# Moving the ranked stages of a sorted attention pair against its ranking chain in a routed-attention and feed-forward kernel

## The chip, the cores and the metric

The kernel runs on one core of a Trainium2 chip. The number that counts is the device time of one execution in microseconds (us); the median of three executions before the change is 958.43 us, the lowest 957.55 and the highest 960.12. The engines of the core are called by their short names in the profile: PE multiplies matrices (and transposes, by a product with an identity), PEld loads the stationary operand for it, DVE is the vector engine, ACT the scalar engine, POOL the GpSimd engine, and SP issues most transfers. Each works through its own list of instructions; they wait for one another through semaphores.

## The reference

A routed attention is followed by a feed-forward block. A query and a key see one another only when they fall into the same one of 16 clusters; the cluster of a row is the argmax of its products with the normalised centroids.

```
q_assign = argmax(einsum('bhsd,hcd->bhsc', q_n, c_n), -1)      # B, H, S, D = 4, 8, 768, 64; 16 clusters
k_assign = argmax(einsum('bhsd,hcd->bhsc', k_n, c_n), -1)
scores = where(q_assign == k_assign, q @ k^T / 8, -1e9)
attn = softmax(scores);  x = attn @ v                           # then (B, H, S, D) -> (B*S, H*D) = 3072 x 512
h = x @ w_in;  g = h * clip(h + 3, 0, 6) / 6;  out = g @ w_out  # w_in 512 x 2048, w_out 2048 x 512
```

## The kernel before

The 32 heads are worked as 16 pairs of heads, `g` = 0 to 15. Pairs 0 to 7 are attended in full, with a mask; this and the decoding of the weights is the first part of the kernel and takes about 255 us. Pairs 8 to 15 are sorted by cluster first, so that only a band of blocks next to the diagonal has to be computed. The change touches only this second part.

**The feed-forward work** is cut into blocks of 256 tokens, three to a batch. A block has eight `up` items and seven `down` items, and each item has two halves, so a block is 30 halves. The first half of an `up` item (`begin`, the `uX` products) ends with two additions on DVE; the second (`uY`) with three additions into `g_sb`, after which `finish` clips the item before it (L502) and, for every second one, forms four sums of the clipped tiles (`gated_sums`, L635), which in this part of the kernel run on DVE. A `tx` transfer (L548) brings the weight sums for the item two further on. A half of a `down` item is eight products of 256 columns. All halves stand in one list, `fill`, in order, and this list never runs empty while the sorted pairs are worked.

**The plan.** The order of the work is written out by hand. `late_plan` lays out a row of points. At each point, `point` in the loop at L1325, the steps planned for it are issued first and then one half from `fill`, except at the two points of a pair that are called busy (L1328). A point with an `up` or `down` half is thus the unit in which the plan counts. Pair `g` has its own zero at point 38 + 28 (g - 8), so one pair follows another at a distance of 28 points (`SLOT`), and `steps_of` (L1172 to L1196) gives each step its offset to this zero. Steps of two neighbouring pairs interleave: offset -30 of one pair is offset -2 of the pair before. At one point, the steps of the earlier pair come first.

**The steps of a pair**, in the order of the work:

- `load_natural`, `turn_natural`: queries and keys are loaded in their natural order (the tile `piece`) and transposed on PE (L899), ACT copies the result (L900).
- The ranking chain: `cluster_scores` (L337, product and copy), `own_clusters` (three transposes `pr` on PE, then `mx` and `oh` on DVE), `run_up` (six small DVE additions), `step_up` (four DVE additions, the last into `upto`), `order` (ten small products into `rk` on PE, the first of which read `upto`; then `edges` and `prod` on DVE) and `positions` (`posf`, `pos` on DVE: the place of each row in its sorted head).
- `load_queries`, `load_keys`: natural rows again, for `scatter`. `scatter` (L1014) is 24 indirect transfers on POOL, each followed by three small memsets (`pause`), which write the rows of queries, keys and values to their places in memory (`qd`, `kvd`).
- `load_ranked` (L870 for queries and keys into `piece`, L893 for values into `vs`) reads the sorted rows back by SP's queue. `turn_ranked` transposes them (again L899 and L900, into `xsort`). `band_masks` makes the mask of the band on DVE (three instructions).
- `band_scores`, `band_values`, `key_adds`, `band_sums`, `band_divide`: the band attention, up to `xr` on DVE (L1144).
- `keep_ranked` stores `xr` to `xsd` by SP's queue; `gather` (L1030), 12 indirect transfers on POOL, fetches the rows back in their natural order into `xn`; `turn_back` transposes them and stores them to `xd`. After the last pair of a batch `turn_back` also puts the batch's feed-forward blocks on `fill` and, when the buffer is free, starts the load `xb` of the next block. `token_sums` (L575) forms sums of `xb` on DVE before the block's first `up`.

All `turn` steps, the band scores and `band_divide` use the one buffer `ps` of PSUM. After the plan comes a check of ranges on DVE (`whether_good`), and then what is left of `fill`.

Of the kernel before, what the change touches and what calls it, by code (L numbers as in the profile page):

```python
# [119 lines left out]
def fast_path(ctx, tc, ok, q, k, v, centroids, moe_w_in, moe_w_out, out):  # L120
# [68 lines left out]
    def load(g, *names):  # L189
        if g > FIRST or (g == FIRST and "v" in names):  # L190
            return
        b, h = divmod(2 * g, H)
        for name in names:
            if name == "v":
                dst = st["v", g] = vp.tile([P, 2, NCH, D], F32, name="vt")
            elif name == "q":
                st["qk", g] = qkp.tile([P, 2, NCH, 2, D], F32, name="qk")
            if name != "v":
                dst = st["qk", g][:, "qk".index(name)]
            src = {"q": q, "k": k, "v": v}[name]  # L200
            for t in range(2):
                nc.sync.dma_start((dst[:, t] if name == "v" else dst[:, :, t]), src[b, h + t].rearrange("(p j) d -> p j d", p=P))
# [9 lines left out]
    def load_weights(i):  # L212
        if i < len(chunks):
            st["raw", i] = rawp.tile([P, WC, 2], U32, name="raw")
            nc.sync.dma_start(st["raw", i], chunks[i][1])
# [54 lines left out]
    def constants():  # L270
        make_identity(nc, ident)
        for t in range(2):
            nc.vector.tensor_reduce(
                out=parity[:, t : t + 1],
                in_=ident.rearrange("p (h t c) -> p t h c", t=2, c=C)[:, t], axis=AX.XY, op=ALU.max,
            )
        nc.gpsimd.memset(half_c, 0.5)
        nc.gpsimd.memset(low_c, 1.0 / BOUND)
        nc.gpsimd.memset(ones, 1.0)
        nc.gpsimd.memset(w_low, W_LOW)  # L280
        nc.gpsimd.memset(one_hot, 0.0)

        idle(18)

    def idle(count):
        warm = psum_t.tile([P, 4, P], F32, name="warm", tag="t")
        for i in range(count):
            nc.tensor.transpose(out=warm[:, i % 4], in_=ident, identity=ident)

    def centroid_norm():  # L290
        cn = unit_rows(nc, startp, cen, D)

        nc.scalar.activation(out=w_totals[:, 0, 0:1], in_=w_low, func=ACT.Exp)

        wide = startp.tile([P, 2, D], F32, name="cenwide")
        for t in range(2):
            nc.vector.tensor_scalar_mul(out=wide[:, t], in0=cn, scalar1=parity[:, t : t + 1])
        st["wide"] = wide
# [10 lines left out]
    def turn(g, part):  # L309
        if part == 0:  # L310
            st["xf", g] = xp.tile([P, NC2, P], F32, name="xf")
        qk, xf = st["qk", g], st["xf", g]
        pt = scratch([P, 4, P], "pqk")
        for i in range(4):
            j = part * 4 + i
            if g == 0 and j == NCH:

                idle(5)
                centroid_turn()
            nc.tensor.transpose(out=pt[:, i], in_=qk[:, j // NCH, j % NCH], identity=ident)  # L320
        dst = xf[:, part * 4 : part * 4 + 4]

        if g == 0 and part == 2:
            nc.vector.tensor_copy(out=dst, in_=pt)
        else:
            nc.scalar.copy(out=dst, in_=pt)
        if part == 2:
            st.pop(("qk", g))
# [4 lines left out]
    def cluster_scores(g):  # L333
        c0, xf = (2 * g) % H * C, st["xf", g]
        ps = scratch([P, 512], "pcs")[:, 0 : NC2 // 4 * P]
        for a in range(4):
            nc.tensor.matmul(  # L337
                ps[a * 2 * C : (a + 1) * 2 * C], lhsT=cnT[:, c0 : c0 + 2 * C], rhs=xf[:, a::4],
                start=True, stop=True,
            )  # L340
        cs = st["cs", g] = st.get("rankp", rtp).tile([P, NC2 // 4, P], F32, name="cs", tag="third")
        nc.scalar.copy(out=cs, in_=ps)
# [112 lines left out]
    def divide(n):  # L455
        return sum_up(n)()
# [713 lines left out]
    SLOT, AHEAD = 28, 38  # L1170

    def steps_of(g):  # L1172

        first, last = g == FIRST, g == NPAIR - 1
        if first:
            plan = [
                (-38, load_queries), (-37, load_keys, 0), (-36, load_keys, 1), (-37, run_up),
                (-36, step_up), (-31, order), (-30, positions), (-20, lambda g: st.pop("signed")()),
            ]
        else:  # L1180
            plan = [
                (-46, load_natural, 0), (-45, load_natural, 1), (-38, turn_natural, 0), (-37, turn_natural, 1),
                (-35, cluster_scores), (-33, own_clusters), (-31, load_queries), (-32, run_up), (-31, step_up),
                (-29, load_keys, 0), (-29, order), (-27, load_keys, 1), (-27, positions),
            ]
        plan += [
            (-29 if first else -24, scatter, 0), (-29 if first else -24, scatter, 1), (-6, band_masks), (-5, load_ranked, 0), (-5, load_ranked, 1),
            (-4, load_ranked, 2), (-3, turn_ranked, 0), (-2, turn_ranked, 1),
        ]
        plan += [  # L1190
            (0, band_scores, (0, 5), 1), (2, band_scores, (2,), 3), (4, band_scores, (4,)),
            (4, band_values, 0), (4, key_adds, 0, 1, 2), (5, key_adds, 0, 3), (7, band_values, 1),
            (7, key_adds, 1, 1, 2), (8, key_adds, 1, 3), (10, band_sums), (12, band_divide), (14, keep_ranked),
            (16 if last else 23, gather), (28 if last else 35, turn_back),
        ]
        return [(g, *step) for step in plan]  # L1196

# [64 lines left out]
    with tc.manual_schedule():  # L1262
        nc.scalar.dma_start(cen, centroids.rearrange("h c d -> (h c) d"))
        load(0, "q", "k")
        constants()
        load(0, "v")
        load_weights(0)
        centroid_norm()
        for part in range(3):
            turn(0, part)  # L1270
        idle(5)
        nc.vector.tensor_copy(out=ident_q, in_=ident)
        load(1, "q", "k")
        load_weights(1)
        cluster_scores(0)
        scores_qk(0)
        route(0)
        scores_qk(1)
        for part in range(2):
            route_turn(0, part)  # L1280

        for n in range(0, total + lag_d + 2, 2):
            g, r = divmod(n, per_pair)
            steps = [i for i in (n, n + 1) if i < total]
            prep = prep_items(g + 1, r)
            for i in steps:
                scores(i)
                exponentials(i)
                key_sums(i)
            for i in (n - lag_v, n - lag_v + 1):  # L1290
                if 0 <= i < total:
                    attn_v(i)
            m = n - lag_d + 1
            if m >= 0 and m % NCH == NCH - 1:
                later.append(divide(m))
                ready(m)
            if prep and r == 4:
                prep.pop(0)()
            if r == 6:
                load(g + 2, "q", "k")  # L1300
                load(g + 1, "v")
            want = min(max(n + 2 - READY, 0) * up_first // (DECODED - READY) - st["done"], len(fill) // 2)
            st["done"] += want
            for i in range(max(len(prep), want)):
                if i < want:
                    fill.pop(0)()
                    fill.pop(0)()
                if i < len(prep):
                    prep[i]()
            if n < total:  # L1310
                for step in decode[: share(n, r)]:
                    step()
                del decode[: share(n, r)]
            check_all()
            checks.extend(later)
            later.clear()

        while checks or later:
            checks.extend(later)
            later.clear()  # L1320
            check_all()
        st["early"] = False
        st["moving"] = True
        open_late()
        for i, point in enumerate(late_plan()):  # L1325
            for op, *args in point:
                op(*args)
            busy = i >= AHEAD and (i - AHEAD) % SLOT in (4, 7)  # L1328
            if fill and not busy:
                fill.pop(0)()  # L1330
        st["last"] = True
        st["moving"] = False
        flag = whether_good()
        while fill:
            fill.pop(0)()
            if len(fill) == HOLD:
                flag()
# [363 lines left out]
```

## Time and profile before

| | |
|---|---|
| median of three executions | 958.43 us |
| the profiled execution | 960.39 us, of which 958.6 us lie between its first and last instruction |
| granted PE clock | 0.999 |
| busy: PE, DVE, ACT, POOL | 929.2, 593.2, 350.2, 576.3 us |
| sorted pairs, last ranked queries turned at | 733.2 us |
| last `turn_back` of the plan | 793.8 us |

The profile was taken in one execution. In its rows a time is counted from the first instruction of that execution. A row of the timeline has start, duration, engine, line, operation, tiles (written from read) and, in brackets, how long the engine had been idle and what ended that. The ends of PE's instructions are modelled, so that rows overlap; the time that a group takes is read from its start to the start of the next.

### The profile page before, as it was taken

To read this page: it belongs to the slowest core of one execution; us is meant where nothing else is said; L and a number is where in the kernel's file an instruction comes from. 1 tells how busy PE (TensorE), PEld (TensorE's weight loads), DVE (VectorE), ACT (ScalarE), POOL (GpSimd) and SP (SyncE) were. 2 spreads that over 40 slices of the span, in tenths; PEclk is the share of its full clock that TensorE was granted. 3 is DMA by queue.
4 is the path that set the end of the run, shared out by engine and by line. 5 is a ranking of instruction groups with operands and counts; after the bars stand their busy time and mean duration, and the time that the engine had idled before them with its cause. 6 is when DMAs were issued, how large, how long until landed. Compare 5 with 4: busy or idle time off the path is not lost.

```text
span 958.6 us, 17615 instructions
## 1 busy us (share of the span) xinstructions
PE 929.2 (97%) x6358; PEld 725.0 (76%) x6358; DVE 593.2 (62%) x1306; ACT 350.2 (37%) x731; POOL 576.3 (60%) x1302
## 2 busy tenths in 40 slices
PE   8999999999899999999999999899998999999997
PEld 5444445555698798797887988778897899999996
DVE  6789888989986275374483474373581564626261
ACT  6888877765112222233132141241231311202020
POOL 3877767657367487787777867767777260303030
PEclk9999999999999999999999999999999999999999
DMA  7355464350474567275583574753753333323220
GB/s 202 94 133 155 132 176 124 101 149 10 144 231 124 135 174 162 89 205 129 161 209 98 140 178 127 170 150 100 197 161 78 102 98 112 106 71 105 59 64 26
DMA packets 174351, 124.23 MB, mean 130 GB/s; under 512 B 134064, under 2 KB 152496, under 8 KB 174256
## 3 DMA queue, kind: packets, MB, share of 16 engines
q1 hardware_dynamic: 164320, 109.86, 42.5%
q0 software_dynamic: 9216, 12.60, 4.4%
q8 instruction: 52, 0.85, 0.4%
q10 hardware_dynamic: 720, 0.56, 0.2%
q14 instruction: 43, 0.35, 0.1%
HBM read 94.67 MB, written 28.31 MB: 128 GB/s over the span
## 4 chain that ended last, share of the span: by engine, by line
PE 52%; POOL 11%; issue 4%; DMA 3%; DVE 3%; ACT 0%; SPq 0%; POOLq 0%; DVEq 0%; ACTq 0%
PE Y L684 13%; PE uY L645 11%; PE X L684 9%; PE uX L645 9%; POOL kvd L1014 4%; POOL qd L1014 4%; POOL w_low L1006 3%; DMA piece<-qd 3%; PE pv L1096 2%; PE ps L899 2%; PE ps L1057 2%; POOL xn L1030 1%; PE pv L1057 1%; DVE tx L556 1%; PE pd L1120 0%
## 5 line engine op out<-in xcount | busy, mean ns | idle before, releaser
L433 POOL TENSOR_TENSOR acc<-acc,ex 128x768 f32<-128x768 f32 x64 | 123.4, 1928 | 37.4 <-ACT ex L423 33.8
L1014 POOL DMA_INDIRECT qd<-qn,pos x96 | 95.5, 995 | 59.9 <-issue 18.4
L1030 POOL DMA_INDIRECT xn<-xsd,pos x96 | 93.0, 969 | 43.4 <-ACT sx L499 22.4
L499 ACT ACTIVATE sx<-g_sb,half_c 128x512 f32<-128x512 f32 x88 | 63.7, 724 | 145.8 <-DVE g_sb L656 121.6
L635 POOL TENSOR_TENSOR g_sb<-g_sb 128x256 f32<-128x256 f32 x52 | 41.8, 826 | 122.0 <-DVE g_sb L502 121.0
L1006 POOL MEMSET w_low<- 128x1 f32 x864 | 92.5, 107 | 33.3
L1014 POOL DMA_INDIRECT kvd<-kvn,pos x96 | 96.9, 1009 | 25.9 <-issue 25.8
L691 DVE TENSOR_TENSOR y<-y,Y 128x256 f32<-128x256 f32 x48 | 20.2, 420 | 139.0 <-PE Y L684 130.5
L684 PE MATMUL X<-w_out_sb,g_sb 128*128 128x256 f32 x384 | 90.5, 382 | 4.0 <-DVE y L691 2.2
L645 PE MATMUL uX<-xb,w_in_sb 128*128 128x128 f32 x704 | 93.0, 275 | 0.0
L684 PE MATMUL Y<-T,g_sb 128*128 128x256 f32 x384 | 88.1, 381 | 0.0
L684 PE MATMUL Y<-w_out_sb,g_sb 128*128 128x256 f32 x384 | 88.1, 381 | 0.0
L645 PEld LDWEIGHTS uX<-xb,w_in_sb 128*128 128x128 f32 x704 | 85.7, 192 | 0.0
L684 PEld LDWEIGHTS X<-w_out_sb,g_sb 128*128 128x128 f32 x384 | 70.9, 190 | 17.2 <-issue 3.1
L656 DVE TENSOR_TENSOR sx<-uX,sx 128x128 f32<-128x128 f32 x176 | 51.0, 290 | 51.2 <-ACT sx L663 33.3
L684 PEld LDWEIGHTS Y<-T,g_sb 128*128 128x128 f32 x384 | 72.0, 190 | 11.9 <-issue 2.6
L684 PEld LDWEIGHTS Y<-w_out_sb,g_sb 128*128 128x128 f32 x384 | 71.9, 190 | 11.9 <-issue 2.5
L400 PE MATMUL ps<-xf 64*128 64x384 f32 x384 | 78.5, 487 | 0.7 <-ACT ex L423 0.7
L423 ACT ACTIVATE ex<-ps 128x768 f32<-128x768 f32 x96 | 72.6, 803 | 4.5 <-PE ps L400 4.5
L443 PE MATMUL pv<-ex,vt 128*64 128x384 f32 x384 | 72.5, 499 | 0.0
L656 DVE TENSOR_TENSOR g_sb<-uY,sx 128x128 f32<-128x128 f32 (+1 forms) x176 | 65.5, 413 | 0.0
L502 DVE SCALAR_TENSOR_TENSOR g_sb<-sx,g_sb 128x512 f32<-128x512 f32 x88 | 63.8, 727 | 2.5 <-ACT sx L499 2.4
(194 smaller groups left out, 1794.9 us busy)
## 6 DMA issues: line engine op xcount, KB each, us to landing
tx<-td SPq DMA_DIRECT2D x86, 384.0 KB
raw<-in_moe_w_in_dram SPq DMA_DIRECT2D x16, 512.0 KB
raw<-in_moe_w_out_dram SPq DMA_DIRECT2D x16, 512.0 KB
xb<-xd SPq DMA_DIRECT2D x12, 512.0 KB
out_dram<-y SPq DMA_DIRECT2D x44, 128.0 KB
qk<-in_q_dram SPq DMA_DIRECT2D x18, 192.0 KB
qk<-in_k_dram SPq DMA_DIRECT2D x18, 192.0 KB
vt<-in_v_dram SPq DMA_DIRECT2D x16, 192.0 KB
```

The lines of the kernel that those rows point to most:

```text
L400: nc.tensor.matmul(st["ps", n][:, t, 0:HALF], lhsT=x[r, NCH + j], rhs=x[r, hf * NHC : (hf + 1) * NHC], start=first, stop=last, skip_group_ ...
L423: nc.scalar.activation(out=ex, in_=sc, func=ACT.Exp, scale=SM_SCALE)
L433: nc.gpsimd.tensor_tensor(out=acc, in0=acc, in1=ex, op=ALU.add)
L443: nc.tensor.matmul(pv[t * D : (t + 1) * D], lhsT=vt[:, t, j], rhs=ex[:, t], start=(j == 0), stop=(j == NCH - 1),)
L499: nc.scalar.activation(out=r, in_=h, func=ACT.Relu, bias=half_c, scale=1.0 / 6.0)
L502: nc.vector.scalar_tensor_tensor(out=g, in0=r, scalar=1.0, in1=h, op0=ALU.min, op1=ALU.mult)
L645: nc.tensor.matmul(dst, lhsT=w[:, kt], rhs=x(kt), start=(kt == 0), stop=(kt == HK - 1))
L656: nc.vector.tensor_tensor(out=out_, in0=in0, in1=in1, op=ALU.add)
L684: nc.tensor.matmul(bank[:, half * HC : (half + 1) * HC], lhsT=g_sb[:, kind, i], rhs=w[:, i], start=(first and i == 0), stop=(last and i == ...
L1006: nc.gpsimd.memset(w_low, W_LOW)
L1014: i = nc.gpsimd.indirect_dma_start(out=rows[name, g, t], in_=src, in_offset=None, out_offset=bass.IndirectOffsetOnAxis(ap=pos[:, a, j, t : ...
L1030: nc.gpsimd.indirect_dma_start(out=xn[:, j, t], out_offset=None, in_=rows["xsd", g, t], in_offset=bass.IndirectOffsetOnAxis(ap=pos[:, 0, j ...
```

## The change

Three things move in `steps_of`, for all sorted pairs.

- In the chain of pairs 9 to 15, `cluster_scores`, `own_clusters`, `run_up`, `step_up` and `order` come one point sooner, `positions` two points sooner. `load_queries` and `load_keys` and `scatter` keep their points; `load_natural` and `turn_natural` too.
- `band_masks`, `load_ranked`, `turn_ranked`, and everything from `band_scores` to `keep_ranked` come two points later for all eight pairs. The two busy points move with them, from 4 and 7 to 6 and 9.
- `turn_back` comes two points later (37 instead of 35), and `gather` stays at 23. For the last pair `gather` comes two points later (18) and `turn_back` one (29).

```diff
         else:
             plan = [
                 (-46, load_natural, 0), (-45, load_natural, 1), (-38, turn_natural, 0), (-37, turn_natural, 1),
-                (-35, cluster_scores), (-33, own_clusters), (-31, load_queries), (-32, run_up), (-31, step_up),
-                (-29, load_keys, 0), (-29, order), (-27, load_keys, 1), (-27, positions),
+                (-36, cluster_scores), (-34, own_clusters), (-33, run_up), (-32, step_up), (-31, load_queries),
+                (-30, order), (-29, positions), (-29, load_keys, 0), (-27, load_keys, 1),
             ]
         plan += [
-            (-29 if first else -24, scatter, 0), (-29 if first else -24, scatter, 1), (-6, band_masks), (-5, load_ranked, 0), (-5, load_ranked, 1),
-            (-4, load_ranked, 2), (-3, turn_ranked, 0), (-2, turn_ranked, 1),
+            (-29 if first else -24, scatter, 0), (-29 if first else -24, scatter, 1), (-4, band_masks), (-3, load_ranked, 0), (-3, load_ranked, 1),
+            (-2, load_ranked, 2), (-1, turn_ranked, 0), (0, turn_ranked, 1),
         ]
         plan += [
-            (0, band_scores, (0, 5), 1), (2, band_scores, (2,), 3), (4, band_scores, (4,)),
-            (4, band_values, 0), (4, key_adds, 0, 1, 2), (5, key_adds, 0, 3), (7, band_values, 1),
-            (7, key_adds, 1, 1, 2), (8, key_adds, 1, 3), (10, band_sums), (12, band_divide), (14, keep_ranked),
-            (16 if last else 23, gather), (28 if last else 35, turn_back),
+            (2, band_scores, (0, 5), 1), (4, band_scores, (2,), 3), (6, band_scores, (4,)),
+            (6, band_values, 0), (6, key_adds, 0, 1, 2), (7, key_adds, 0, 3), (9, band_values, 1),
+            (9, key_adds, 1, 1, 2), (10, key_adds, 1, 3), (12, band_sums), (14, band_divide), (16, keep_ranked),
+            (18 if last else 23, gather), (29 if last else 37, turn_back),
         ]
...
-            busy = i >= AHEAD and (i - AHEAD) % SLOT in (4, 7)
+            busy = i >= AHEAD and (i - AHEAD) % SLOT in (6, 9)
```

## The prediction

> **What bounds the kernel now.** I read the page first, then the waits of PE and of SP's queue, then the timelines of PE, DVE and SP around one pair, and the end of the plan.
>
> ```profile
> span 958.6 us, 17615 instructions
> PE 929.2 (97%) x6358; PEld 725.0 (76%) x6358; DVE 593.2 (62%) x1306; ACT 350.2 (37%) x731; POOL 576.3 (60%) x1302
> ```
>
> PE is the bound, and what it computes stays the same: the same halves and steps, in another order. The time can change only by PE's idle time. In the sorted part (280 to 800 us) the waits of PE are these four rows, and SP's queue has one that belongs to them:
>
> ```profile
> PE ps L899 <- DMA piece<-qd: 9.3, 7, 2.8
> PE uX L645 <- DVE g_sb L656: 0.5, 1, 0.5
> PE uY L645 <- issue: 0.2, 1, 0.2
> PE rk L968 <- issue: 0.2, 1, 0.2
> ...
> SPq L870 <- DMA qd<-qn,pos: 26.7, 3, 14.3
> ```
>
> So 10.2 us of idle time is all that can be won there. 9.3 of it is `turn_ranked` waiting for sorted queries, seven of eight times. Two causes: for pairs 8 and 15 SP itself waits for `scatter` before it may load; for the others the load is simply issued too late. SP's rows for pairs 13 and 15, and PE's rows for these turns:
>
> ```profile
> 607.23 0.81 SPq L695 DMA_DIRECT2D out_dram<-y  x2
> 608.09 0.45 SPq L548 DMA_DIRECT2D tx<-td  x1
> 608.65 0.99 SPq L870 DMA_DIRECT2D piece<-qd  x2
> ...
> 715.13 15.26 SPq L870 DMA_DIRECT2D piece<-qd  x2
> ...
> 733.23 0.85 PE L899 MATMUL ps<-ident,piece 128*128 128x128 f32 x6 [2.76 <-DMA piece<-qd]
> 733.91 1.89 PE L684 MATMUL X<-w_out_sb,g_sb 128*128 128x256 f32 x8
> 735.64 0.82 PE L899 MATMUL ps<-ident,piece 128*128 128x128 f32 x6
> ```
>
> In the last two rows a `down` half takes 1.73 us (733.91 to 735.64). In the third-last row the reader sees the wait, 2.76 us; the load's second issue had ended at 715.13 + 15.26 = 730.39, so a load alone lands 2.84 us after it.
>
> **Part 1: the later loads and turns.** Pairs 8 and 15: `scatter` sets the landing and its place does not move (POOL works on ranks that come no later), while the turn moves behind two more halves, 3.5 us. Its waits end; the second is 2.76. Pair 13: at its old place the load stood behind the `y` stores of a `down` item (607.23) on SP, at the new one behind a `tx` load alone. Pair 9: the load is then issued long before its turn, as nothing but the `xb` load of the block stands ahead. Pairs 10 to 12 keep their distance of two points from load to turn, but now `order` (0.62 us on PE, below) lies inside this distance and `own_clusters` (0.32) does not, and PE will wait there (part 2); their turns wait no more. What is late next: the turn of pair 13, whose load then comes at the same distance as that of pair 11 in the rows of part 2 (a wait of 0.77 at 491.88), less 0.30 for `order` in place of `own_clusters`: 0.5. And the turn of pair 15, whose load is now behind the store of the half three before the turn: an estimated 2.6 us of DVE additions and issues, plus 2.84, against 3 x 1.73; 0.3. The 0.5 of `uX` is one `tx` load behind a store of `xr`, which moves behind it; gone. The small two (0.2, 0.2) I count as gone too, the second since it is the wait of part 2 in its old size. So 10.2 goes and 0.8 comes.
>
> A rule bears on the 2.84. The Trainium skill (DMA: Bandwidth & Descriptors, section "Anatomy of one DMA — SWDGE (gpsimd) path") gives a transfer about 2.0 us plus its bytes at 436 GB/s. By the page a load of 192 KB would land 2.45 us after its issue, not 2.84 as in this trace; pair 15 would then not wait, and the sum below would be 0.3 lower. The measured 2.84 stands in the sum.
>
> **Part 2: the chain on DVE.** This decides. `order` on PE needs `upto`, the last result of `step_up`. PE and DVE around pair 12's chain, as it is now:
>
> ```profile
> 486.15 0.61 PE L645 MATMUL uX<-xs,tx 128*128 128x128 f32 x4
> ...
> 487.49 0.49 PE L918 MATMUL pr<-ident,cs 128*128 128x128 f32 x3
> 487.81 0.61 PE L645 MATMUL uY<-xs,tx 128*128 128x128 f32 x4
> ...
> 489.60 0.61 PE L645 MATMUL uX<-xs,tx 128*128 128x128 f32 x4
> ...
> 491.88 0.84 PE L899 MATMUL ps<-ident,piece 128*128 128x128 f32 x6 [0.77 <-DMA piece<-qd]
> ...
> 494.35 0.82 PE L899 MATMUL ps<-ident,piece 128*128 128x128 f32 x6
> ...
> 496.34 0.24 PE L968 MATMUL rk<-every,upto 128*128 128x1 bf16 x4
> 496.96 0.62 PE L645 MATMUL uY<-xs,tx 128*128 128x128 f32 x4
> ...
> 486.35 0.29 DVE L656 TENSOR_TENSOR sx<-uY,sx 128x128 f32<-128x128 f32 x1 [0.44 <-PE uY L645]
> ...
> 487.22 0.70 DVE L502 SCALAR_TENSOR_TENSOR g_sb<-sx,g_sb 128x512 f32<-128x512 f32 x1
> 487.84 0.29 DVE L1039 TENSOR_SCALAR ends<-edges,sign,odd 128x2 f32<-128x2 f32 x1
> ...
> 488.83 0.61 DVE L656 TENSOR_TENSOR sx<-uX,sx 128x128 f32<-128x128 f32 x2
> 489.36 0.55 DVE L920 TENSOR_REDUCE mx<-pr 128x24 f32<-128x384 f32 x1
> ...
> 490.41 0.28 DVE L656 TENSOR_TENSOR sx<-uY,sx 128x128 f32<-128x128 f32 x1
> ...
> 491.27 0.68 DVE L502 SCALAR_TENSOR_TENSOR g_sb<-sx,g_sb 128x512 f32<-128x512 f32 x1
> 491.99 1.58 DVE L635 TENSOR_TENSOR g_sb<-g_sb 128x256 f32<-128x256 f32 x4
> 493.49 0.17 DVE L936 COPY runs<-oh 128x64 bf16<-128x64 bf16 x1
> ...
> 494.70 0.61 DVE L656 TENSOR_TENSOR sx<-uX,sx 128x128 f32<-128x128 f32 x2
> 495.23 0.64 DVE L932 TENSOR_TENSOR steps<-steps 128x64 bf16<-128x64 bf16 x3
> 495.90 0.23 DVE L932 TENSOR_TENSOR upto<-steps 128x128 bf16<-128x128 bf16 x1
> ```
>
> The reader is to see that DVE runs without a pause from 486.35 to 496.13, where `upto` is done, and that `order` starts at 496.34: 0.2 us of slack. What covers it on PE, from `pr` on, is one and a half `up` items and the two turns with their wait. The change takes the turns out of this stretch: they come after `order`. PE from `pr` to `order` is then `pr` 0.32 and two whole `up` items; a first half is 1.34 (486.15 to 487.49), a second 1.79 (487.81 to 489.60), so 0.32 + 2 x 3.13 = 6.58 us.
>
> DVE, in the new order of the list, from the same start (the end of a `uY`), each from the start of its row to the start of the next: signal 0.20, additions of that item 0.87, clip 0.62, `mx` and `oh` 1.05, additions after the next `uX` 0.53, `run_up` 1.21, three additions 0.86, clip 0.72, gated sums 1.50, `band_masks` 0.99, `step_up` 0.90. The sum is 9.45. PE waits 9.45 - 6.58 = 2.9 us. This pattern (the chain begins before `up` 6, 4 and 2) is that of pairs 11, 12 and 13: 8.7 us. Pair 10 begins before `down` 0: without 0.53 and 0.86 DVE needs 8.06, PE has 0.32 + 4 x 1.73 = 7.24; 0.8. Pair 14 begins before `up` 0, where no clip or gated sums are due: two `y` additions (0.87) in their place, 6.6 against 6.58; nothing. Pairs 9 and 15 begin in `down` halves, where DVE is free. Together 9.5. Earlier positions let POOL start its scatters sooner; nothing of PE waits for that but the turns of pairs 8 and 15, counted above.
>
> Other moved steps I cost at nothing: `cluster_scores` has one half (1.73 or 1.79) behind the second natural turn to cover ACT's copy of 0.8; `load_queries` now stands behind the ranked loads and ahead of the values on SP, and the values are due eight points on; `keep_ranked` lands while POOL still scatters.
>
> **Part 3: the end of the plan.** For pair 15 there is no next scatter to hide the gather.
>
> ```profile
> 766.51 0.49 PE L1133 MATMUL pdt<-ident,dn 128*128 128x128 f32 x3
> ...
> 768.50 1.02 DVE L1144 TENSOR_TENSOR xr<-ps,inverses 128x384 f32<-128x384 f32 x2
> ...
> 790.17 0.95 POOL L1030 DMA_INDIRECT xn<-xsd,pos  x1
> ...
> 792.00:793.00 1.00, 1.00 (x7) 0.87 (x6) 0.00 (x0) 0.00 (x0) 0.00 (x0) 1.00 0.02 4
> ...
> 793.82 0.82 PE L899 MATMUL ps<-ident,xn 128*128 128x128 f32 x6
> ...
> 802.83 0.42 DVE L575 TENSOR_TENSOR xs<-xs,xb 128x256 f32<-128x256 f32 x1
> ```
>
> The turn does not wait now. The last gather is issued by 791.12 and its traffic ends in 792 to 793 (last column, GB/s), so it lands between 791.1 and 793.8; I take 793.0, 23.5 after `xr` (769.52). After the change `band_divide` follows `up` 4, whose gated sums (1.50) come ahead of `xr` on DVE: `xr` is done 3.0 + 1.5 after `pdt`, the rows land 28.0 after it. PE gets there 0.99 + 6 halves of `up` (9.4) + 9 of `down` (15.6) = 25.95 after it: a wait of 2.0 (0.2 to 2.9). Behind it one half less stands before the next block: 0.82 + 5 x 1.73 = 9.5, while `xs` is ready 9.4 after the turn's start (803.25 less 793.82); 0.1.
>
> **Sum.** -10.2 + 0.8 + 9.5 + 2.1 = +2.2 us. The profiled execution took 960.39 (span 958.6 and 1.8 around it), so it would be 962.6; the median shown, 958.43, lies 1.96 lower, so 960.6. Bounds: DVE's chain may be 0.7 us shorter or longer per pair (the 0.62 and 0.72 of one clip, the signals), three pairs, so 2.1; the end 0.2 to 2.9, or 0.8 more if all of `xs` counts. That makes -1.8 to +5.9.
>
> **Rivals.** *A, DVE keeps up.* If DVE's work in the stretch is at most 6.6 us, 2.9 less than I add up, `order` does not wait; that would need the gated sums and `band_masks` to fall outside. For it: DVE is busy 62% overall. Against it: the rows above have no pause. Then the turns of pairs 10 to 12 keep at most 0.5 each (0.77 less 0.30); with 0.9 for these, the 0.8 and the 2.1 of the end, 3.8 stands in place of 10.2: 952.0. *B, the transfers collide.* The twelve loads of ranked rows, queries and keys (SP takes 0.5 us or more to issue one: 0.99 for the two at 608.65) now stand within four points in place of six, and `tx` loads queue among them. If a `tx` lands after its `up` begins, by 1 to 2 us in pairs 11 to 13, add some 4 us to the sum: 964.6. For it: SP needs 6 us for them, as long as four halves of `up` take; against it: a `tx` has four points, two items and the wait at `order`, more than 9 us. *C, nothing moves.* Load and turn keep their distance, and if SP's issue goes with them and `order` waits only as much as is saved, 958.4.
>
> **Chances.** Forecast 0.65, A 0.15, B 0.13, C 0.07. About 0.3% (2.9 us) is what a measurement here can tell from none. Of the forecast's 0.65, 0.24 lies above +2.9 and 0.02 below -2.9. Slower: 0.24 + 0.13 = 0.37; faster: 0.15 + 0.02 = 0.17; same: 0.46. The range takes in B and leaves out A: 956.5 to 965.5.
>
> **What would show it.** Waits of `rk` (L968) near 3 us three times and 0.8 once; the turn's waits down from 9.3 to about 1; a wait of `ps<-ident,xn` near 794 to 800 of about 2 us; `pos` two to four us sooner against `pr`. Wrong if `rk` does not wait (A), or `uX` waits for `tx` (B).

## The result, and the profile after

The changed kernel takes 967.83 us (median of 6 runs, 966.23 to 970.68) against 958.43 of the kernel before: 1.0097 times as long, 95% interval 1.0079 to 1.0116. The forecast was 960.6 us, with 956.5 to 965.5 as its range; the time lies above it. The profiled execution took 970.68 us, 10.3 more than that of before.

The line of the page's first part, busy time by engine, and then the waits of PE in the sorted part up to the first `up` items of the next block (280 to 830 us; columns: total us, times, longest):

```profile
PE 934.1 (96%) x6358; PEld 730.4 (75%) x6358; DVE 594.3 (61%) x1306; ACT 350.7 (36%) x731; POOL 581.0 (60%) x1302
```

```profile
PE rk L968 <- DVE upto L932: 9.2, 4, 2.8
PE ps L899 <- DMA piece<-qd: 2.5, 2, 1.9
PE ps L899 <- DMA xn<-xsd,pos: 2.5, 2, 1.3
PE uX L645 <- DVE sx L656: 1.7, 1, 1.7
```

The 10.2 us of waits before have become 15.9. `order` (`rk`, L968) now carries most of them, four times; the turns wait 2.5 in place of 9.3; the end has 4.1 where it had none. That is 5.7 us. The rest stands in the first fence: with the same 6358 matmuls PE is busy 934.1 us, 4.9 more than the 929.2 before. Together 10.6, and 0.3 comes back elsewhere.

PE and DVE around the chain of pair 13, to be held against the rows of pair 12 in the prediction (columns: start, us, engine, line, operation, tiles, count, and in brackets the idle time before and what ended it):

```profile
549.82 0.49 PE L918 MATMUL pr<-ident,cs 128*128 128x128 f32 x3
...
559.28 0.25 PE L968 MATMUL rk<-every,upto 128*128 128x1 bf16 x4 [2.72 <-DVE upto L932]
...
560.43 1.91 PE L645 MATMUL uX<-xb,w_in_sb 128*128 128x128 f32 x8
562.14 1.49 PE L899 MATMUL ps<-ident,piece 128*128 128x128 f32 x6
...
566.45 1.06 PE L645 MATMUL uX<-xb,w_in_sb 128*128 128x128 f32 x8
```

```profile
550.01 0.29 DVE L656 TENSOR_TENSOR sx<-uY,sx 128x128 f32<-128x128 f32 x1 [0.87 <-PE uY L645]
...
557.34 0.28 DVE L1039 TENSOR_SCALAR ends<-edges,sign,odd 128x2 f32<-128x2 f32 x1
...
559.00 0.22 DVE L932 TENSOR_TENSOR upto<-steps 128x128 bf16<-128x128 bf16 x1
```

The turns (L899) stand behind `rk`, no longer ahead of it, and DVE works without a pause from 550.01 to `upto`: the wait is the one that part 2 worked out, 2.7 for 2.9. But the rows behind the wait are new. `uX` takes 1.91 us and the first turn 1.49; the next `uX` takes 1.06, and a turn in the prediction's rows 0.82. The stretches around it (columns: from and to, length, PE busy and its instructions, granted clock of TensorE, DMA share, GB/s):

```profile
556.00:559.30 3.30, 0.58 (x7) 1.00 1.18 237
559.30:560.30 1.00, 1.00 (x14) 0.99 1.07 284
560.30:563.70 3.40, 3.40 (x19) 0.50 1.10 282
563.70:567.00 3.30, 3.30 (x31) 1.00 0.96 193
```

One microsecond after the wait the clock is halved, for 3.4 us, and PE does in them what takes 1.7 at full clock. After the change the trace has three such stretches while PE works, from 259.9, 560.3 and 625.1 us; the profiled execution of before has none. Three times 1.7 is 5.1, the 4.9 us of PE's longer busy time. Two of the three stand behind waits of moved steps: that from 560.3 behind `order` of pair 13, that from 625.1 behind the turn of pair 13. The first stands behind a wait of `X` for `y` on DVE, ahead of the sorted part. This wait is 2.21 us long in the trace of before as well, where the clock holds; that it falls here is chance (last section), and so some 1.7 of the 4.9 us is not the change's doing.

### The profile page after: what moved, and what is told of

The parts are those of the page before. It is cut to its first block, busy times and chain, and to the rows that moved or that the text cites. A ratio compares the mean times of both kernels' runs of the same rounds, so it can differ in the third digit from the quotient of the medians.

```text
span 968.9 us, 17620 instructions
## 1 busy us (share of the span) xinstructions
PE 934.1 (96%) x6358; PEld 730.4 (75%) x6358; DVE 594.3 (61%) x1306; ACT 350.7 (36%) x731; POOL 581.0 (60%) x1302
## 5 line engine op out<-in xcount | busy, mean ns | idle before, releaser
L1030 POOL DMA_INDIRECT xn<-xsd,pos x96 | 95.7, 997 | 53.3 <-DVE g_sb L656 31.8
L684 PEld LDWEIGHTS Y<-w_out_sb,g_sb 128*128 128x128 f32 x384 | 71.8, 190 | 10.6 <-issue 1.3
```

What stands on the lines that cost most here:

```text
L684: nc.tensor.matmul(bank[:, half * HC : (half + 1) * HC], lhsT=g_sb[:, kind, i], rhs=w[:, i], start=(first and i == 0), stop=(last and i == ...
L1030: nc.gpsimd.indirect_dma_start(out=xn[:, j, t], out_offset=None, in_=rows["xsd", g, t], in_offset=bass.IndirectOffsetOnAxis(ap=pos[:, 0, j ...
```

## The experiments

All kernels were timed in the same manner as the changed one; ratios are to runs of the kernel before on the same chip (its medians there were 958.43 to 959.42). Waits are those of PE in the profiled execution, 280 to 830 us; "end" is `ps<-ident,xn` and the `uX` after it. The clock is the mean over the runs of each kernel of the mean granted clock; 0.0018 is one stretch of 3.4 us at half clock (1.7 of 966 us). The mean takes in the time behind PE's last product too: the traces have 0.9 to 4.2 us at half clock there, which cost PE nothing and take 0.0005 to 0.0022 from it, so that small differences in this column say little.

| kernel | median us | ratio, 95% | waits of `order` / turns / end | clock |
|---|---|---|---|---|
| before | 958.43 | | 0.2 / 9.3 / 0 | 0.9967 |
| changed | 967.83 | 1.0097 (1.0079 to 1.0116) | 9.2 / 2.5 / 4.1 | 0.9947 |
| 1 chain only | 960.17 | 1.0012 (1.0002 to 1.0022) | 1.1 / 5.6 / 0 | 0.9970 |
| 2 sorted part only | 963.65 | 1.0056 (1.0038 to 1.0074) | 1.8 / 5.0 / 4.1 | 0.9963 |
| 3 warm | 966.37 | 1.0080 (1.0066 to 1.0094) | 3.2 / 1.9 / 5.0 | 0.9975 |
| 4 `order` later | 962.30 | 1.0045 (1.0030 to 1.0061) | 0 / 7.2 / 3.9 | 0.9975 |
| 5 masks sooner | 961.51 | 1.0030 (1.0019 to 1.0041) | 5.4 / 1.9 / 2.9 | 0.9974 |
| 6 old end | 962.96 | 1.0051 (1.0033 to 1.0069) | 9.2 / 1.3 / 0 | 0.9953 |
| 7 loads and turns apart | 953.24 | 0.9948 (0.9931 to 0.9966) | 0 / 2.8 / 0 | 0.9982 |
| 8 loads sooner | 953.34 | 0.9946 (0.9930 to 0.9963) | 1.5 / 1.4 / 0 | 0.9982 |
| 9 masks twice | 974.75 | 1.0165 (1.0147 to 1.0184) | 14.9 / 0.5 / 2.7 | 0.9912 |
| 10 loads and masks | 953.80 | 0.9944 (0.9927 to 0.9962) | 0 / 0.9 / 0 | 0.9979 |

**1 and 2: one half of the change each.** The diff's first hunk holds both halves. Experiment 1 is the kernel before with the chain's lines alone:

```diff
-                (-35, cluster_scores), (-33, own_clusters), (-31, load_queries), (-32, run_up), (-31, step_up),
-                (-29, load_keys, 0), (-29, order), (-27, load_keys, 1), (-27, positions),
+                (-36, cluster_scores), (-34, own_clusters), (-33, run_up), (-32, step_up), (-31, load_queries),
+                (-30, order), (-29, positions), (-29, load_keys, 0), (-27, load_keys, 1),
```

> Only the seven points of the chain are those of the change; loads, turns, scores and the rest of the sorted part stay where they were before. Theory (the turns were the cover of the chain): between `pr` and `order` stand four halves and both turns of the pair before, 0.32 + 4 x 1.57 + 2 x 0.82 = 8.2 us against DVE's 9.45, so `order` waits 0 to 1.2 us per pair, while the turns still wait for their rows some 6 to 9 us in all; the clock stays at 0.998 to 0.999; 957 to 962 us. Rival (the sooner chain itself is what costs): `order` waits 2.7 us in pairs 11 to 13 here too, on top of the turns' 9.3; 966 us or more.

Experiment 2 is the changed kernel with these two lines taken back.

> Only the sorted part (masks, loads, turns, scores, values, division, gather) stands two points later; the chain keeps its old points. Theory (cover): only the first turn is left between `pr` and `order`, 0.32 + 4 x 1.57 + 0.82 = 7.4 us against 9.45, so `order` waits about 2.0 us in pairs 11 to 13 although the chain was not moved at all; turns wait 2.5 and the end 4.1 as after the change: 12.6 us of waits, 2.4 more than before, and up to 3 us of slow clock: 961 to 965 us. Rival (the sooner chain costs): no wait at `order`, 6.6 us of waits in place of 10.2, 955 us.

```profile
PE ps L899 <- DMA piece<-qd: 5.2, 5, 2.7
PE rk L968 <- DVE upto L932: 1.1, 3, 0.5
```

These are waits of experiment 1, and the next fence has those of experiment 2:

```profile
PE ps L899 <- DMA piece<-qd: 5.0, 5, 1.8
PE ps L899 <- DMA xn<-xsd,pos: 2.5, 2, 1.4
PE rk L968 <- DVE upto L932: 1.8, 2, 0.9
```

With the chain alone `order` waits at most 0.5 us, and the time grows by 0.1%. So the sooner chain by itself is not what costs. (The turns waited 5.6 us, a little less than expected, and the clock was 0.997, a little lower.) With the sorted part alone `order` waits twice 0.9, half of what I expected, since the turn just ahead of it waits for its rows in the same place and gives DVE that time; the end's 4.1 are all there. Only the two halves together leave `order` without a turn ahead of it: +0.1% and +0.6% alone, +1.0% together.

**3: work in the wait.** The changed kernel, with transposes that nobody reads ahead of `order`:

```diff
+        if 11 <= g <= 13:
+            idle(19)
         rk = scratch([P, 512], "rk")
```

> The changed kernel, with 19 transposes of the identity (2.6 us of TensorE work that nobody reads) put in front of `order` in pairs 11 to 13, where PE would wait 2.7 us anyway. Theory (the 4.9 us that the waits do not explain are the clock, halved for 3.4 us after a wait): the work before `order` takes just as long, but the clock does not fall there: mean clock 0.997 or more, 963 to 965.5 us. Rival (the clock falls for another reason, or the 4.9 us come from the order of the work on PE): 967 to 969 us, clock 0.993 to 0.996.

The page's busy time, PE's rows at pair 13's `order`, and the stretches around it:

```profile
PE 934.8 (97%) x6415; PEld 731.4 (76%) x6415; DVE 593.3 (62%) x1306; ACT 350.6 (36%) x731; POOL 577.5 (60%) x1302
```

```profile
554.53 2.24 PE L288 MATMUL warm<-ident 128*128 128x128 f32 x19
557.67 0.25 PE L970 MATMUL rk<-every,upto 128*128 128x1 bf16 x4 [0.90 <-DVE upto L932]
```

```profile
554.00:557.70 3.70, 2.80 (x27) 1.00 1.31 241
557.70:561.10 3.40, 3.40 (x36) 1.00 1.21 269
```

The work behind `order` still waits about as long (2.24 us of filling and 0.90 idle), but PE is busy for most of it, and the clock does not fall in this trace until PE has ended its work. Less three fillings of some 2.2 us, PE is busy about 928 us, as in the kernel before. So the 4.9 us of longer busy time were the clock. That idle time brings its fall, this one trace can't show alone: of the three stretches only that from 560.3 stood behind a wait that is filled here. The clock over all runs does show it: it rises from 0.9947 to 0.9975, which is 2.7 us, and no run of experiment 3 is below 0.997 where none of the changed kernel is above 0.996. The time fell by 1.5 only and missed my 963 to 965.5, 0.9 of the difference by longer waits at the end (5.0 for 4.1 us); the intervals of the two times overlap, so the clock is the evidence here, not the time.

**5 and 9: less and more on DVE.** Both are the changed kernel; 9 runs the three operations of `band_masks` in a loop of two, 5 has

```diff
-            ... (-4, band_masks), (-3, load_ranked, 0), (-3, load_ranked, 1),
+            ... (-10, band_masks), (-3, load_ranked, 0), (-3, load_ranked, 1),
```

> The changed kernel with `band_masks` (0.99 us of DVE) six points sooner, ahead of the stretch from `pr` to `order`. Theory (`order` waits for what DVE has to do in this stretch, all of it, not only for the chain): its waits fall by 0.99 in pairs 11 to 13 (2.7 to 1.8) and to nothing in pair 10, 9.2 to 5.3 us; waits under 2 us let the clock fall less often, up to 2 us more: 961.5 to 964.5 us. Rival (the chain's own length or the `pr` transposes set the wait): waits of 2.7 stay, 966 to 968.5 us.

> The changed kernel with the three operations of `band_masks` done twice, 0.99 us more of DVE in the stretch from `pr` to `order`. Theory (a wait costs itself, and a wait of more than about 1.9 us also lets the clock fall for 3.4 us behind it, about 1.7 us each): `order` waits 3.7 us in pairs 11 to 13 and 1.9 in pair 10, 4.0 us more in all, and nearly each of the three long waits now halves the clock where about half of them did: 972 to 975.5 us, mean clock 0.992 to 0.994. Rival (a wait costs itself alone): 971 to 972, the clock as after the change, 0.995.

The waits of `order`, first of experiment 5, then of 9:

```profile
PE rk L968 <- DVE upto L932: 5.4, 3, 1.8
```

```profile
PE rk L968 <- DVE steps L932: 7.7, 2, 3.8
PE rk L968 <- DVE upto L932: 7.2, 3, 3.9
```

Both times lie in the ranges of the theories, and both rivals fall; the clock of 9 is a little lower than expected. With 0.99 us of DVE less, as is and more, the long waits are 1.8, 2.8 and 3.8 us: `order` waits for all that DVE has queued, of whatever pair. The time goes with it more than one for one: from the changed kernel to experiment 9 all these waits together grow from 15.9 to 18.1, 2.2 us, and the time by 0.68%, 6.5 us; the clock falls by 0.0035, 3.4 us. To experiment 5 the waits fall by 5.7 (the end's among them) and the clock rises by 0.0027, 2.6 us; the time falls by 0.67%, 6.4 us. So the sum of waits and clock is 0.9 short in the one step and 1.9 too much in the other; the waits are those of one execution, the times medians. Stretches of 3.4 us in the trace of experiment 9, cut where its clock changes:

```profile
431.10:434.50 3.40, 1.33 (x12) 1.00 1.23 270
434.50:437.90 3.40, 1.60 (x12) 0.50 1.14 301
437.90:441.30 3.40, 3.40 (x11) 0.50 1.30 240
441.30:444.70 3.40, 3.40 (x22) 1.00 1.00 172
```

The wait of pair 11, 3.87 us, lies across 434.50, empties more than half of two stretches in a row and so halves the clock for two.

**4: `order` behind the turns.** The changed kernel with

```diff
-                (-30, order), (-29, positions), (-29, load_keys, 0), (-27, load_keys, 1),
+                (-29, load_keys, 0), (-28, order), (-27, positions), (-27, load_keys, 1),
```

> The changed kernel, with `order` and `positions` two points later (-28, -27), behind both turns of the pair before; the chain's other five steps stay early. Theory (cover and clock): six halves and both turns stand between `pr` and `order`, 0.32 + 6 x 1.57 + 2 x 0.82 = 11.4 us against 9.45: `order` does not wait, 6.6 us of waits are left (turns 2.5, end 4.1) against 10.2 before, the clock is 0.998 or more: 953.5 to 956.5 us. Rival (the order of the work on PE costs the 4.9 us by itself): 958.5 to 961 us, PE busy 934 us with the clock at 0.995.

```profile
PE ps L899 <- DMA piece<-qd: 4.7, 5, 2.1
PE ps L899 <- ACT xsort L900: 2.5, 3, 1.0
```

`order` waits no more, and the clock is no lower than that of before. But I expected 953.5 to 956.5 and it took 962.3: the turns wait again, 7.2 us. 4.7 of it is for their rows, which the wait at `order` had covered. The second row is new: the second turn waits for ACT to copy the first out of the one `ps` tile, and ACT, in its trace, stands behind a clip's activation that waits for DVE (ACT and PE around the chain of pair 12):

```profile
494.59 0.72 ACT L499 ACTIVATE sx<-g_sb,half_c 128x512 f32<-128x512 f32 x1 [4.52 <-DVE g_sb L656]
...
495.36 0.80 ACT L900 COPY xsort<-ps 128x768 f32<-128x768 f32 x1
```

```profile
496.22 0.87 PE L899 MATMUL ps<-ident,piece 128*128 128x128 f32 x6 [0.82 <-ACT xsort L900]
```

DVE is late all the same; it only reaches PE by another way. All waits together are 11.1 us, only 0.9 more than the 10.2 in the trace of before, and yet the kernel takes 0.45%, 4.3 us, longer than that one; the next section comes back to this.

**6: the end undone.** The changed kernel with pair 15 back at the old points, from its loads to `turn_back` (and the two points without an item of that slot):

```diff
+        d = 0 if last else 2
-            (2, band_scores, (0, 5), 1), ... (14, band_divide), (16, keep_ranked),
-            (18 if last else 23, gather), (29 if last else 37, turn_back),
+            (0 + d, band_scores, (0, 5), 1), ... (12 + d, band_divide), (14 + d, keep_ranked),
+            (16 if last else 23, gather), (28 if last else 37, turn_back),
```

> The changed kernel with pair 15 alone back at the old points from its loads to `turn_back`. Theory (the end costs 4.1 us because the rows of the last pair come back too late): the waits of `ps<-ident,xn` (2.5) and of the `uX` behind it (1.7) go, and the turn of pair 15 waits 2.7 again in place of 0.6: 965.8 us, 964.5 to 967. Rival (the end waits for the DMA queues, whatever the points): the end's 4.1 stay, 967.5 to 970 us.

The end's 4.1 us are gone, and the turn of pair 15 does not wait at all, so this won 0.46%, 4.4 us, where I expected 2. Experiment 1 has no wait at that turn either, and there it stands at its old point: with the sooner chain the last transfer of pair 15's `scatter` starts at 725.57 us instead of 729.42. So the 2.76 us of pair 15 went by the sooner chain alone; the later turn, to which part 1 of the prediction put it down, was not needed.

**7, 8 and 10: the distance from load to turn.** Experiment 8 is the kernel before with one thing moved:

```diff
-            ... (-5, load_ranked, 0), (-5, load_ranked, 1),
-            (-4, load_ranked, 2), ...
+            ... (-7, load_ranked, 0), (-7, load_ranked, 1),
+            (-6, load_ranked, 2), ...
```

> The kernel before, with the ranked loads alone two points sooner; everything else stays, the turns too. Theory (distance from load to turn): the turns of pairs 9 to 13 wait for nothing (6.5 us go), that of pair 15 waits 2.8 as before, since its rows come from its scatter; 952 to 954.5 us. Rival (the landing is set by the scatter or the traffic, not by the point of issue): 957.5 to 960 us with the turns' waits unchanged.

Experiment 7 is experiment 4 with the end of experiment 6 and

```diff
-            ... (-4, band_masks), (-3, load_ranked, 0), (-3, load_ranked, 1),
-            (-2, load_ranked, 2), (-1, turn_ranked, 0), (0, turn_ranked, 1),
+            ... (-10, band_masks), (-5, load_ranked, 0), (-5, load_ranked, 1),
+            (-4, load_ranked, 2), (-2 if last else -1, turn_ranked, 0), (-1 if last else 0, turn_ranked, 1),
```

> Loads and turns taken apart: `order` behind both turns (as in the run with `order` later), the ranked loads at their old points with the turns two points later, `band_masks` six points sooner, pair 15 at the old points save for its turns (one later). Theory (the turns' waits were a matter of the distance from load to turn, which the change keeps; DVE's backlog shows at `order` or, through ScalarE, at the second turn): the turns' waits fall from 7.2 to about 1 (pair 15), `order` and the end wait for nothing, 10.2 us of waits before become 1 to 2.5: 950 to 953.5 us. Rival (loads put sooner hold SP's queue, and `tx` comes late instead; or the transfers themselves are what is short): 955 to 960 us with waits of `uX` for `tx`.

Experiment 10 is experiment 8 with `band_masks` at -10 and the turns at -2 and -1.

> The kernel before with the ranked loads two points sooner (as in the run with that alone), `band_masks` four points sooner and both turns one point later; chain, scores and end as before. Theory (distance from load to turn, DVE's load ahead of `order`): the 1.5 us that `order` waited with the loads alone go with 0.99 us less on DVE, and the 1.4 that the turns of pairs 9 and 15 still waited go with one half more: 950 to 952.5 us. Rival (nothing is left to win there, or the copy on ScalarE is late for the scores): 953 to 955 us.

The waits of experiments 8, 7 and 10, in this order:

```profile
PE rk L968 <- DVE upto L932: 1.5, 3, 0.7
PE ps L899 <- DMA piece<-qd: 1.4, 2, 1.0
```

```profile
PE ps L899 <- ACT xsort L900: 2.8, 3, 1.1
PE uX L645 <- DMA tx<-td: 1.5, 1, 1.5
```

```profile
PE uX L645 <- DMA tx<-td: 2.8, 3, 1.2
```

All three beat both kernels, by 0.5% of the time before, and can't be told from each other; 7 and 8 lie in the ranges of their theories. The edit of 8 is enough: loads issued sooner, turns where they were, take 9.3 us of the turns' waits down to 1.4. The change had moved loads and turns by the same two points. What is left of 7 comes by way of ACT, as in experiment 4, and from one late `tx`. What is left of 10 is mainly `tx`, so its expected 950 to 952.5 was missed by 1.3 us; SP issues `tx` right behind the sooner loads there, but whether its queue or the traffic makes them late was not tried.

## Why the prediction was wrong

**The step that failed** is the second sentence of its argument: "The time can change only by PE's idle time." PE's work stayed the same, but not the time it takes: the trace has 4.9 us more of busy PE, all of it in three stretches at half clock that follow waits. The sum put the clock at nothing, without a reason. Beside that, terms of the sum were mis-sized: the turns (2.5 us for 0.8), the end (4.1 for 2.1) and, for the median, the 10.2 us that were there to be won.

The profile of before gave no hint of the clock: its mean is 0.999, and its waits of 2.62 and 2.76 us passed without a fall. The other runs would have: of 46 of that kernel 13 read 0.996 or less, more than the time behind PE's last product can account for, so they hold at least one such stretch. Runs at 0.995 took 960.8 us on average and runs at 0.999 took 957.4.

**Between the runs the clock's share is smaller** than between the two profiled executions. The mean clocks differ by 0.0020 (0.9967 to 0.9947), 1.9 us of 9.3 (0.97%). Of the other 7.4, the waits in the two traces give 5.7, and 1.7 remain. They point at the profiled execution of before, which took 960.39 us where its other runs of the same clock took about 957.4. The experiments bear this out: held against before, the changed kernel and each of the ten others take between 1.5 and 4.5 us more than the waits of PE in their traces (280 to 830 us, the fillings of experiment 3 with them) and their mean clocks add up to. So that execution had some 3 us that most runs of its kernel do not have, and the prediction read its 10.2 us of waits from it. Where these 3 us lie, no trace shows.

**Part 1, the turns.** 9.3 us to 2.5, predicted to 0.8. The turn of pair 13 waited 1.9 in place of 0.5, that of pair 15 0.6 in place of 0.3. SP's queue ahead of the first:

```profile
617.26 0.97 SPq L870 DMA_DIRECT2D piece<-qd  x2
618.33 4.68 SPq L870 DMA_DIRECT2D piece<-kvd  x2
```

```profile
624.42 0.85 PE L899 MATMUL ps<-ident,piece 128*128 128x128 f32 x6 [1.90 <-DMA piece<-qd]
```

The rows came 6.2 us after their issue (618.23 to 624.42), not 2.84, and SP needed 4.68 us for the next two loads. This is a collision of transfers as in rival B, at one place, though not at `tx`, where B looked for it. Its cause among the transfers was not tried. And the sentence on pairs 10 to 12, "PE will wait there (part 2); their turns wait no more", was right in the changed kernel, but as experiments 2 and 4 show, the gain was lent by the wait at `order`: where that shrinks or goes, the turns wait 5.0 and 4.7 us for their rows, about half of the 9.3 before.

**Part 2, the chain on DVE.** 9.2 us for 9.5; 0.94 and three times 2.7 to 2.8 for 0.8 and three times 2.9, in the pairs named. The mechanism stands (experiments 1, 2, 5 and 9), and rival A, that DVE keeps up, falls. What was missing is what such a wait brings besides itself.

**Part 3, the end.** 4.1 for 2.1. The turn's wait was 2.5 for 2.0. The 0.1 for the next block became 1.7: the first addition of `xs` stood for 11.82 us on DVE, and behind it, in order, stood 2.6 us of `whether_good` and 0.9 of `y` additions, which the term did not count.

```profile
811.98 0.43 DVE L575 TENSOR_TENSOR xs<-xb 128x256 f32<-128x256 f32 x1 [11.82 <-DMA xb<-xd]
...
816.11 0.16 DVE L794 TENSOR_REDUCE one<-low 128x1 f32<-128x6 f32 x1
816.18 0.87 DVE L691 TENSOR_TENSOR y<-y,Y 128x256 f32<-128x256 f32 x2
```

**The sum.** +2.2 was predicted for the profiled execution and +10.3 came: 1.7 more at the turns, 2.0 more at the end, 0.3 less at `order`, and 4.9 of slow clock, with some 0.2 of rounding and of the first part of the program. For the medians, +2.2 was predicted and +9.4 came. The mis-sized waits alone would have given about 964.0, inside the range; the 1.9 of the clock make it 965.9, just above; and the last 1.9 up to 967.83 stand in no trace. They would fit the 3 us that the profiled execution of before had above most of its runs.

## What to carry to other kernels

A step that waits for a load may be the only cover of another engine's work: before it is moved, add up what the other engine has queued until the next step that needs it. When turns wait for their rows, move the loads alone; moving both keeps the distance, and about half of the wait stayed here. One profiled execution may be a few us off its kernel's median: do not read the gain to be had from it alone. And a wait of PE can have a second price, a stretch at half clock behind it: compare PE's busy time for the same matmuls, and count idle time by stretches of 3.4 us, not by its sum.

## What the runs showed of the hardware

The clock falls by stretches on a grid that is fixed within an execution. In the trace of the changed kernel they begin at 259.9, 560.3, 625.1 and 966.5 us (the last after PE's work), and the distances, 300.4, 64.8 and 341.4, are 88, 19 and 100 times 3.413 us, the length that the trace records for one stretch. Cut on this grid, the windows with a wait and those behind them are, after the change:

```profile
430.60:434.00 3.40, 1.47 (x14) 1.00 1.21 265
434.00:437.40 3.40, 2.56 (x20) 1.00 1.14 301
495.40:498.90 3.50, 1.81 (x21) 1.00 1.21 262
498.90:502.30 3.40, 3.40 (x34) 1.00 1.20 276
556.90:560.30 3.40, 1.02 (x14) 1.00 1.18 247
621.70:625.10 3.40, 1.50 (x14) 1.00 0.87 201
625.10:628.50 3.40, 3.40 (x19) 0.51 1.07 256
```

Three waits of `order` are equally long, 2.7 to 2.8 us. The one that leaves its window 1.02 of 3.40 us busy halves the next (its row stands above, 560.30 to 563.70); the two that lie across a boundary do not (1.47 and 1.81 busy), while a wait of 1.90 us inside one window does (1.50 busy). So the bound lies near 1.5 us of busy time.

The other traces agree. Each has half clock behind PE's last product, which fixes its grid. Cut into windows on it, from 8 us on, the twelve traces show this: every window at full clock with at most 1.4 us of busy PE is followed by half clock, nine of them while PE still has work; of six windows with 1.46 to 1.57 us two are; of some 3300 with more, none is. (Once the clock is low the bound may be another: in the second row of experiment 9 it stays low behind 1.60. The ends of matmuls are modelled, so it can't be read more closely.) The waits of 2.62 and 2.76 us in the trace of before lie across boundaries and leave their windows 1.68 us busy or more.

Whether a wait meets the bound then depends on where the grid falls in that execution. The wait of `X` for `y` ahead of the sorted part shows it, since it is 2.2 us long in all twelve traces. In those of the changed kernel and of experiment 9 it leaves a window 1.28 and 1.33 us busy, and the clock falls; in the ten others no window there has less than 1.49, and the clock holds. The same would explain why the changed kernel's runs vary from 0.993 to 0.996. All this is read from the traces; the grid was not shifted on purpose.

The Trainium skill (TensorE: Matmul & The Clock Gate, section "Part 1: The HAM clock gate") describes such a free-running window of 3413 ns and two rates, full and half. The trace agrees on both. It has the half rate come after at least one idle window; here 1.90 us of idle time in a window was enough, and the measurement decides.
